# Windowed attention and a mixture of experts: the last token group's second GEMM by Strassen's scheme

## The chip, the cores and the metric

The kernel runs on one core of one Trainium2 chip. The metric is device time in microseconds of one execution, the median of the runs shown. TensorE (PE in the rows, PEld for its weight loads) does matrix products into PSUM; VectorE (DVE), ScalarE (ACT) and GpSimd (POOL) do the elementwise work; SyncE (SP) issues the DMAs.

## What is computed

The reference, cut to its core (batch 4, 8 heads, 576 tokens, head size 64; 2304 tokens of width 512; 4 experts with hidden width 1024):

```python
scores = scale * np.matmul(q, k.transpose(0, 1, 3, 2))
mask = (rel >= 0) & (rel < 64)
attn = softmax(np.where(mask, scores, -1e9))
x = np.matmul(attn, v).transpose(0, 2, 1, 3).reshape(2304, 512)
p = domain_probs / (domain_probs.sum(-1, keepdims=True) + 1e-9)
for e in range(4):
    h = np.maximum(x @ w1[e], 0.0)
    out += p[:, e:e + 1] * (h @ w2[e])
```

Every expert is applied to every token. Inputs and outputs are float32.

## The kernel before

**Precision.** Every big product is made of float32r operands in two parts: a rounded high part, and a low part, the rest. A product of 128 rows of weights is three matmuls: high x high, high x low, low x high.

**Groups and units.** The 2304 tokens are three groups of 768 (NGRP, numbered 0 to 2), each computed as two halves of 384 (T). The 4 x 1024 hidden columns are 16 units of 256 (NU), two row blocks of 128 each. So there are 48 units, `i` from 0 to 47; two neighbours are a pair. Attention for a group (18 steps of 128 tokens in all) runs beside the units of the group before; group 0's own attention is the start.

**First GEMM.** For a unit, the hidden values are a 2 x 2 block product (halves of the 512 input columns, halves of the hidden columns, halves of the tokens), done by Strassen's scheme in Winograd's form: seven products P1 to P7 (PROD, line 220 ff.), each six matmuls of 384 columns (L674). The combinations of x (B11, T1 and so on) are made once for a group, those of w1 for each unit (POOL, L536), and each is split into high and low (ACT L549, DVE L553). The products go to three PSUM banks: P1 and then P2 to X, P6, P7 and P4 to Y, P5 and P3 to V. P1 is copied to SBUF as s1 (ACT, L696); then DVE adds: u2 = Y + s1, u3 = Y + s1, c22 = V + u3, c21 = Y + s1, c12 = V + u2 (L693). The four results pass a relu and a split (`hidden`: ACT L600, DVE L603). The first two units are computed without Strassen (DIRECT). The order of the products in a unit is ORDER (P1, P6, P5, P7, P2, P4, P3), and FIRST (P1, P5, P2, P6, P7, P4, P3) in unit 2 and in the first and last unit of each group.

**Second GEMM.** For a pair and each of the group's six blocks of 128 tokens, y has 128 tokens x 512 columns: 6 matmuls of 512 columns for each of the two units (`gemm2`, L758), so 12 blocks of six a pair. w2 is loaded for each unit, cast and split (ACT L569, POOL L575). DVE adds p x y to an accumulator (L779), and after a group's last pair it is stored. The very last token block is done in two halves of 256 columns (`final`, L612 to L637).

**Order.** TensorE's steps stand in a list (`seq`): the products of a unit with a y block between each two, the y blocks two units behind. All other work has a due place against that list; a planner (`Planner.order`) that knows costs, buffers and the port that DVE and POOL share sets the order on every engine before the program is built. Each engine then runs its list in order, and waits at semaphores.

Of the kernel before, what the change touches and what calls it, by code (L numbers as in the profile page):

```python
# [44 lines left out]
class Planner:  # L45
# [5 lines left out]
    def order(self):  # L51
# [15 lines left out]
        while left:  # L67
# [60 lines left out]
def kernel(ctx: ExitStack, tc: tile.TileContext, q, k, v, dprobs, w1, w2, out):  # L128
    nc = tc.nc
    P = 128  # L130
    W = 64
    N, DM = out.shape
# [12 lines left out]
    NU = w1.shape[0]  # L145
    UPE = NU // E
# [17 lines left out]
    slots.update(X=["b0"], Y=["b1"], V=["b2"], D=["b0", "b1", "b2"], y=["b3", "b4"], pa=["b5", "b6", "b7"])  # L164
# [91 lines left out]
    for u in range(NG // 2):  # L256
# [66 lines left out]
        for c in range(2):  # L323
# [21 lines left out]
            else:  # L345
# [170 lines left out]
    w1p, w1_done, w2p, w2_done = {}, {}, {}, {}  # L516
    PIECES = (("w1a", 0, 2), ("w1b", 2, 4), ("w1c", 4, 6), ("w1d", 6, 7))
    COMBS = ((2, 1, 5, ALU.add), (3, 0, 1, ALU.subtract), (1, 2, 0, ALU.subtract), (6, 4, 1, ALU.subtract))
    for i in range(nun):
        ui = i % NU  # L520
        due = at["p", i, "P1"] - 7 if i >= DIRECT else -100 + 10 * i
        raw = Buf("w1r")

        def load_w1(on, i=i, ui=ui, b=raw):
            t = make(b, f"w1r{i}")
            nc.sync.dma_start(t[:, 0:2], w1[ui, :, 0:2])
            nc.sync.dma_start(t[:, 4:6], w1[ui, :, 2:4])

        ld = add(f"lw1_{i}", dict(SP=dma(524288)), load_w1, due - 14, takes=[raw])

        made = {}
        step = ld
        for dst, x, y, op in COMBS if i >= DIRECT else ():
            def comb_w1(on, b=raw, dst=dst, x=x, y=y, op=op):
                t = b.tile
                nc.gpsimd.tensor_tensor(out=t[:, dst], in0=t[:, x], in1=t[:, y], op=op)  # L536
# [353 lines left out]
```

## Time and profile before

| | |
|---|---|
| runs (us) | 836.97, 835.76, 837.24; median 836.97 |
| profiled execution: span | 833.3 us (the page gives no time of its own beside it) |
| TensorE busy | 816.3 us, 98% |
| DVE, ACT, POOL busy | 560.1, 355.4, 332.3 us (67%, 43%, 40%) |
| the chain that ended last | PE 93%, DVE 5% |
| costliest lines | L758 (second GEMM) 47% of the chain, L674 (first GEMM) 40% |
| DMA | 89.78 MB, mean 108 GB/s |

The span runs from the first to the last instruction; the timed runs are a little longer. Matmuls overlap in their pipeline, so the time of one is read from start to start. "Idle before" names what ended an engine's wait.

### The profile page before, as it was taken

To read this page: it belongs to the slowest core of one execution; us is meant where nothing else is said; L and a number is where in the kernel's file an instruction comes from. 1 tells how busy PE (TensorE), PEld (TensorE's weight loads), DVE (VectorE), ACT (ScalarE), POOL (GpSimd) and SP (SyncE) were. 2 spreads that over 40 slices of the span, in tenths; PEclk is the share of its full clock that TensorE was granted. 3 is DMA by queue.
4 is the path that set the end of the run, shared out by engine and by line. 5 is a ranking of instruction groups with operands and counts; after the bars stand their busy time and mean duration, and the time that the engine had idled before them with its cause. 6 is when DMAs were issued, how large, how long until landed. Compare 5 with 4: busy or idle time off the path is not lost.

```text
span 833.3 us, 13433 instructions
## 1 busy us (share of the span) xinstructions
PE 816.3 (98%) x5020; PEld 725.4 (87%) x5020; DVE 560.1 (67%) x966; ACT 355.4 (43%) x811; POOL 332.3 (40%) x339
## 2 busy tenths in 40 slices
PE   7988999999999999999999999999999999999998
PEld 6876988988888889888888888888889889889887
DVE  5868866665766797487688677588556566566553
ACT  5746535344453363464344443444353333333320
POOL 4744524344334254343435434425433433433400
PEclk8999999999999999999999999999999999999999
DMA  9633434343444235354343415114213113113102
GB/s 330 229 96 109 131 98 138 103 152 108 127 134 126 76 112 164 111 149 143 105 129 96 133 39 152 56 46 140 89 50 102 52 51 100 52 51 102 29 23 76
DMA packets 53521, 89.78 MB, mean 108 GB/s; under 512 B 8016, under 2 KB 20560, under 8 KB 53456
## 3 DMA queue, kind: packets, MB, share of 16 engines
q1 hardware_dynamic: 53312, 88.53, 33.4%
q8 instruction: 39, 0.64, 0.3%
q10 hardware_dynamic: 144, 0.39, 0.1%
q14 instruction: 26, 0.21, 0.1%
HBM read 77.89 MB, written 11.01 MB: 107 GB/s over the span
## 4 chain that ended last, share of the span: by engine, by line
PE 93%; DVE 5%; POOL 1%; issue 1%; ACT 0%; DMA 0%; DVEq 0%; POOLq 0%; ACTq 0%
PE y L758 47%; PE Y L674 17%; PE V L674 12%; PE X L674 11%; PE vb L436 2%; PE sb L311 2%; DVE T L479 1%; PE tb L386 1%; PE warm_out L801 1%; DVE h L603 0%; DVE w1c L553 0%; PE yl L627 0%; DVE B L479 0%; DMA qb<-in_q_dram 0%; ACT sm L339 0%
## 5 line engine op out<-in xcount | busy, mean ns | idle before, releaser
L758 PE MATMUL y<-w2s,h 128*128 128x512 f32 x1716 | 443.0, 394 | 1.4 <-POOL w2s L575 1.0
L758 PEld LDWEIGHTS y<-w2s,h 128*128 128x128 f32 x1716 | 317.5, 188 | 54.2 <-POOL w2s L575 1.8
L575 POOL TENSOR_TENSOR w2s<-w2r,w2s 128x512 fp32r<-128x512 f32 x96 | 134.1, 1409 | 212.5 <-ACT w2s L569 202.7
L536 POOL TENSOR_TENSOR w1r<-w1r 128x256 f32<-128x256 f32 x184 | 150.1, 821 | 168.5 <-DMA w1r<-in_moe_w_dram 143.9
L693 DVE TENSOR_TENSOR u<-Y,s 128x384 f32<-128x384 f32 x92 | 51.1, 555 | 124.1 <-PE Y L674 124.0
L779 DVE SCALAR_TENSOR_TENSOR acc<-y,dp,acc 128x512 f32<-128x512 f32 x125 | 93.1, 745 | 20.8 <-PE y L758 20.6
L603 DVE SCALAR_TENSOR_TENSOR h<-c,h 128x384 fp32r<-128x384 f32 x138 | 82.2, 603 | 15.8 <-ACT h L600 15.5
L600 ACT ACTIVATE h<-c 128x384 fp32r<-128x384 f32 x138 | 72.1, 525 | 24.9 <-DVE c L693 24.5
L549 ACT CAST w1b<-w1r 128x512 fp32r<-128x512 f32 x46 | 28.5, 620 | 112.8 <-PE Y L674 112.3
L377 POOL TENSOR_TENSOR sm<-sm,st 128x512 f32<-128x512 f32 x36 | 39.6, 1104 | 92.0 <-DVE st L371 79.7
L569 ACT CAST w2s<-w2r 128x1024 fp32r<-128x1024 f32 x48 | 50.4, 1050 | 25.5 <-PE y L758 21.3
L549 ACT CAST w1a<-w1r 128x512 fp32r<-128x512 f32 x48 | 29.8, 622 | 71.7 <-PE Y L674 66.8
L674 PE MATMUL V<-B,w1d 128*128 128x384 f32 x276 | 56.8, 341 | 1.6 <-DVE c L693 1.6
L674 PE MATMUL Y<-T,w1b 128*128 128x384 f32 x276 | 56.6, 340 | 0.0
L674 PE MATMUL V<-T,w1b 128*128 128x384 f32 x276 | 55.7, 336 | 0.9 <-DVE h L603 0.9
L674 PE MATMUL Y<-T,w1c 128*128 128x384 f32 x276 | 55.5, 336 | 0.8 <-ACT w1b L549 0.8
L674 PE MATMUL X<-B,w1c 128*128 128x384 f32 x276 | 56.2, 339 | 0.0
L674 PE MATMUL X<-B,w1a 128*128 128x384 f32 x276 | 55.4, 334 | 0.5 <-DVE h L603 0.5
L674 PE MATMUL Y<-T,w1a 128*128 128x384 f32 x276 | 55.4, 335 | 0.0
L693 DVE TENSOR_TENSOR c<-Y,s 128x384 f32<-128x384 f32 x46 | 25.5, 555 | 44.0 <-PE Y L674 43.9
L361 ACT ACTIVATE sm<-sm,st 128x128 f32<-128x128 f32 x120 | 46.6, 391 | 19.2 <-DVE st L354 19.0
L674 PEld LDWEIGHTS V<-B,w1d 128*128 128x128 f32 x276 | 49.8, 188 | 5.6 <-DVE c L693 1.9
(85 smaller groups left out, 973.7 us busy)
## 6 DMA issues: line engine op xcount, KB each, us to landing
w1r<-in_moe_w_dram SPq DMA_DIRECT2D x96, 256.0 KB, 3.7
w2r<-in_moe_w_dram SPq DMA_DIRECT2D x48, 512.0 KB, 3.6
vn<-in_v_dram SPq DMA_DIRECT2D x35, 256.0 KB, 3.0
kt<-in_k_dram SPq DMA_DIRECT2D x17, 384.0 KB, 4.9
hop<-tp SPq DMA_DIRECT2D x96, 64.0 KB, 1.8
pt<-hop SPq DMA_DIRECT2D x24, 256.0 KB, 2.9
qb<-in_q_dram SPq DMA_DIRECT2D x18, 256.0 KB, 4.0
out_dram<-acc SPq DMA_DIRECT2D x17, 256.0 KB, 2.0
```

What stands on the lines that cost most here:

```text
L361: nc.scalar.activation(t[:, p, :], t[:, p, :], AF.Exp, bias=st.tile[:, 1, p : p + 1], accum_out=st.tile[:, 2, p : p + 1],)
L377: nc.gpsimd.tensor_tensor(out=sm.tile, in0=sm.tile, in1=rl.to_broadcast([P, NP, P]), op=ALU.mult)
L536: nc.gpsimd.tensor_tensor(out=t[:, dst], in0=t[:, x], in1=t[:, y], op=op)
L549: f(t[:, 0], raw.tile[:, lo_:hi_])
L569: nc.scalar.copy(make(b, f"w2s{i}")[:, 0], raw.tile)
L575: nc.gpsimd.tensor_tensor(out=b.tile[:, 1, f], in0=raw.tile[:, f], in1=b.tile[:, 0, f].bitcast(F32), op=ALU.subtract)
L600: nc.scalar.activation(make(b, f"h{i}_{f}{t_}")[:, 0], src.tile[:, :T], AF.Relu)
L603: nc.vector.scalar_tensor_tensor(out=b.tile[:, 1], in0=src.tile[:, :T], scalar=0.0, in1=b.tile[:, 0].bitcast(F32), op0=ALU.max, op1=ALU.su ...
L674: nc.tensor.matmul(t[:, :T], wb.tile[:, a, wi, ws], cb.tile[:, x, c, :], start=first and m == 0, stop=m == 5, skip_group_check=True,)
L693: return lambda t, p_: nc.vector.tensor_tensor(out=t, in0=p_, in1=o.tile, op=ALU.add)
L758: nc.tensor.matmul(o, hh[:, a, ts], w[:, b, f, :], start=x == 0 and m == 0, stop=x == 1 and m == 5)
L779: nc.vector.scalar_tensor_tensor(out=ab.tile, in0=yb.tile, scalar=pc, in1=ab.tile, op0=ALU.mult, op1=ALU.add)
```

## The change

1. **Second GEMM of group 2, pairs 16 to 22.** It is computed transposed (w2 is the weight operand, the hidden values move) and by the same seven-product scheme over both units of a pair at once: blocks are halves of the 256 hidden columns of a unit, of the 512 output columns and of the 768 tokens. Each product is two blocks (`c`) of six matmuls of 384 columns, `gemm2m` (L993), three a unit. DVE (the first time ACT too) adds each block to one of 14 accumulators M (`gather`, L1007, L1009); the products are not combined until pair 22 is through (`total`).
2. **Weights for it.** While group 1 runs, the sums and differences of w2 that the scheme needs are made for 14 units (`w2_products`: POOL or DVE L607, ACT L614, L617), split and stored to DRAM, seven stores of 256 KB a unit; group 2 loads them, four loads a pair (`load_wp`, L693, L695).
3. **Split w1 kept.** Sixteen units (2 to 17) store w1a to w1d, already split, to DRAM (L574); group 2 loads them (`load_kept`, L561) in place of raw w1, and makes no combinations or splits of w1.
4. **Hidden values of group 2.** `weighted` (L813) applies relu and multiplies with the token's probability, which lies along columns now (probabilities are transposed once on TensorE and kept in DRAM, `prob_rows`); `minus` (L827) makes the differences, `cut` (L797, L800) the splits.
5. **The last pair, 23**, is not by Strassen: `gemm2z` (L1038), 14 blocks of six 384-column matmuls, then 24 of 192 columns. Output of group 2 is stored transposed, in a second tensor that the host turns back.
6. **P1 seeded into PSUM, in all groups.** ACT copies P1 from bank X into bank Y (L920) and P6, P7 and P4 accumulate there. So u2 and u3 are ACT copies out of Y, c21 is Y itself, and DVE has c22 and c12 left. P6 now waits for the seed.
7. The exps of the masked attention steps are two steps of two heads each instead of one of four; steps may be held back by a `gate` until TensorE's list has come to a place.

The diff, cut to its core:

```diff
+    MORDER = ("P1", "P3", "P7", "P5", "P6", "P2", "P4")
     def g_steps(pair, half):
+        if pair == nun // 2 - 1:
+            if half:
+                return []
+            full = [(dq, t) for t in (1, 0) for dq in range(DM // P)]
+            return [("z", pair, *x, y) for y in range(2) for x in full[:-1]] + [("zf", pair, *full[-1], y) for y in range(2)]
+        if pair >= LAST * NU // 2:
+            steps = [("m", pair, x, c) for x in MORDER for c in range(2)]
+            return steps[:7] if half == 0 else steps[7:]
         return [("g", pair, half * TPB + t, x) for t in range(TPB) for x in range(2)]
...
+    def keep_w1(i, kind, b, after, due):
...
+        def store(on):
+            nc.sync.dma_start(t, b.tile.bitcast(F32))
...
+        if i // NU == LAST:
+            for kind, lo_, hi_ in PIECES:
+                load_kept(i, kind, lo_, hi_, due - 2 + lo_)
...
+        if i // NU == LAST - 1 and ui < NU - 2:
+            w2_products(i, raw2, b2, w2_done[i])
...
-            first = pname in ("P1", "P6", "P5")
+            first = pname in ("P1", "P5")
...
-            elif pname == "P2":
+            elif pname in ("P2", "P6"):
                 after = after + [evac[i, "s1"]]
...
             if pname == "P1":
-                s1 = tmp("s1", lambda t, p_: nc.scalar.copy(t, p_), pb, [s], [], "ACT")
+                yb = bank[i, "Y"] = Buf("Y")
+
+                def seed(on, i=i, yb=yb, pb=pb):
+                    copy(on, make(yb, f"Y{i}")[:, :T], pb.tile[:, :T])
+
+                evac[i, "s1"] = add(f"s1_{i}", COPY, seed, due - 8, [s], [yb], [pb])
             elif pname == "P6":
-                u2 = tmp("u2", addto(s1), pb, [s, evac[i, "s1"]], [s1])
+                u2 = tmp("u2", copy, pb, [s], [], COPY, due=due - 8)
...
             elif pname == "P4":
-                c21 = tmp("c21", addto(s1), pb, [s, evac[i, "s1"]], [s1])
-                hidden(i, 1, 0, c21, [evac[i, "c21"]], due + 3, ("DVE",))
+                if i // NU == LAST:
+                    hidden_last(i, 1, 0, pb, [s], due, False)
+                else:
+                    hidden(i, 1, 0, pb, [s], due - 4)
...
+            def gemm2m(on, mb=mb, ww=ww, y=y, units=units, pname=pname, c=c, pair=pair):
+                o = make(mb, f"m{pair}{pname}{c}")
+                m = 0
+                for u, i in enumerate(units):
+                    for a, x in ((0, 0), (0, 1), (1, 0)):
+                        nc.tensor.matmul(
+                            o[:, :T], ww.tile[:, y, u, a, c * P : (c + 1) * P], hs[i, pname].tile[:, x], start=m == 0, stop=m == 5
+                        )
+                        m += 1
```

**The order on the engines.** TensorE, unit 40 of group 2, from its P1. Before (X, Y, V are the banks of the products, y the second GEMM, h the hidden values):

```order
L674 MATMUL X40_7111<-B11_2_5874,w1a_40_7018 128x384 x6
L758 MATMUL y19_0_7122<-w2s38_6895,h38_00_6945 128x512 x3
L758 MATMUL y19_0_7122<-w2s38_6895,h38_10_6967 128x512 x3
L674 MATMUL Y40_7141<-T2_2_5946,w1a_40_7018 128x384 x6
L758 MATMUL y19_0_7122<-w2s39_7087,h39_00_7077 128x512 x3
L758 MATMUL y19_0_7122<-w2s39_7087,h39_10_7100 128x512 x3
L674 MATMUL V40_7159<-T1_2_5897,w1b_40_7054 128x384 x6
```

and of the change (m19P10: pair 19, product P1, block 0; hs the split hidden values, wp the loaded w2 products):

```order
L899 MATMUL X40_7663<-B11_2_6298,w1a_40_7534 128x384 x6
L993 MATMUL m19P10_7677<-hs38P1_7456,wp19_0_7443 128x384 x3
L993 MATMUL m19P10_7677<-hs39P1_7613,wp19_0_7443 128x384 x3
L899 MATMUL Y40_7684<-T2_2_6377,w1a_40_7534 128x384 x6
L993 MATMUL m19P11_7701<-hs38P1_7456,wp19_0_7443 128x384 x3
L993 MATMUL m19P11_7701<-hs39P1_7613,wp19_0_7443 128x384 x3
L899 MATMUL V40_7715<-T1_2_6320,w1b_40_7563 128x384 x6
```

Between two products there is one block of six again; it has 384 columns instead of 512, and seven instead of six stand in a unit.

ACT around the copy of P1 at the start of unit 41 (of unit 40 before). Before:

```order
L549 CAST w1c_40_7095<-w1r40_6863 128x512
L600 ACTIVATE h39_10_7100<-c21_39_7097 128x384
L549 CAST w1d_40_7118<-w1r40_6863 128x256
L696 COPY s1_40_7132<-X40_7111 128x384
L600 ACTIVATE h39_01_7138<-c12_39_7120 128x384
```

and of the change (t40P5 is a difference of hidden values, hs40P5 its split):

```order
L797 CAST hs40P7_7816<-t40P7_7803 128x384 [waits Pool_49]
L797 CAST hs40P5_7828<-t40P5_7818 128x384 [waits DVE_49,Activation_49]
L920 COPY Y41_7839<-X41_7820 128x384 [waits PE_49]
L797 CAST hs40P2_7856<-c12_40_7812 128x384 [waits DVE_49]
L920 COPY u2_41_7867<-Y41_7839 128x384 [waits PE_49,Activation_49]
```

The copy writes a PSUM bank now, and the instruction ahead of it waits for DVE.

DVE in the change, from c12 of unit 40 on (MP50: accumulator of P5, block 0):

```order
L917 TENSOR_TENSOR c12_40_7812<-V40_7715,u2_40_7710 128x384 [waits PE_49]
L827 TENSOR_TENSOR t40P5_7818<-r4010_7794,c22_40_7753 128x384 [waits DVE_49]
L800 TENSOR_TENSOR hs40P7_7816<-t40P7_7803,hs40P7_7816 128x384 [waits Activation_49]
L827 TENSOR_TENSOR t40P6_7830<-r4000_7772,t40P5_7818 128x384 [waits DVE_49]
L800 TENSOR_TENSOR hs40P5_7828<-t40P5_7818,hs40P5_7828 128x384 [waits Activation_49]
L797 CAST hs40P6_7842<-t40P6_7830 128x384 [waits DVE_49]
L813 SCALAR_TENSOR_TENSOR c12_40_7812<-c12_40_7812,pb21_7646 128x384
L800 TENSOR_TENSOR hs40P6_7842<-t40P6_7830,hs40P6_7842 128x384 [waits DVE_49]
L827 TENSOR_TENSOR t40P4_7865<-c12_40_7812,t40P6_7830 128x384 [waits DVE_49]
L800 TENSOR_TENSOR hs40P2_7856<-c12_40_7812,hs40P2_7856 128x384 [waits Activation_49]
L1009 TENSOR_TENSOR MP50_6877<-m19P50_7805,MP50_6877 128x384 [waits PE_49]
```

Before, DVE had adds, subtractions of w1 and h, and three drains of y here, some 16 instructions a unit. From this c12 to that of unit 41 there are 24: c22 and c12, four weightings (two read PSUM), two casts, three differences, six subtractions and seven gathers. POOL has the fourth difference and the seventh subtraction. On SP, w1d of a unit waits for TensorE (P3 of the unit before), and w1a and w1b of the next unit stand behind it.

## Rows read from the trace of the kernel before

**Rows 1.** The view of the cores, and the chain's shares by engine (page).

```profile
core 0: 833.3 us, clock 0.994
...
PE 93%; DVE 5%; POOL 1%; issue 1%; ACT 0%; DMA 0%; DVEq 0%; POOLq 0%; ACTq 0%
```

**Rows 2.** Windows of groups 1 and 2: length, then busy time (instructions) per engine, clock, DMA.

```profile
296.00:561.00 265.00, 264.63 (x1601) 234.92 (x1600) 191.52 (x325) 118.24 (x272) 109.48 (x109) 1.00 0.36 110
561.00:812.00 251.00, 251.00 (x1251) 225.79 (x1250) 152.39 (x255) 95.00 (x168) 95.48 (x92) 1.00 0.21 70
```

**Rows 3.** Timeline of TensorE in group 2: start, length, engine, line, operation.

```profile
656.68 1.20 PE L674 MATMUL X<-B,w1a 128*128 128x384 f32 x6
657.72 1.55 PE L758 MATMUL y<-w2s,h 128*128 128x512 f32 x6
659.11 1.21 PE L674 MATMUL Y<-T,w1a 128*128 128x384 f32 x6
...
672.35 1.20 PE L674 MATMUL X<-B,w1a 128*128 128x384 f32 x6
```

**Rows 4.** Timeline of TensorE early in group 0.

```profile
91.60 1.21 PE L674 MATMUL Y<-T,w1b 128*128 128x384 f32 x6
...
95.79 1.21 PE L674 MATMUL X<-B,w1a 128*128 128x384 f32 x6
```

**Rows 5.** Timeline of TensorE at the end.

```profile
813.39 13.80 PE L758 MATMUL y<-w2s,h 128*128 128x512 f32 x60
827.03 3.03 PE L627 MATMUL yl<-w2s,h 128*128 128x256 f32 x24
```

**Rows 6.** Timeline around two s1 copies: one on time, the latest.

```profile
657.97 0.48 ACT L696 COPY s<-X 128x384 f32<-128x384 f32 x1 [0.61 <-PE X L674]
...
658.88 1.12 PEld L674 LDWEIGHTS Y<-T,w1a 128*128 128x128 f32 x6
...
625.33 1.20 PE L674 MATMUL X<-B,w1a 128*128 128x384 f32 x6
...
627.50 0.46 ACT L696 COPY s<-X 128x384 f32<-128x384 f32 x1
```

**Rows 7.** Groups of instructions in group 1, DVE and POOL: shapes, count, busy us, mean ns, idle before.

```profile
L603 DVE SCALAR_TENSOR_TENSOR h<-c,h 128x384 fp32r<-128x384 f32 x48 | 28.3, 600 | 4.4 <-ACT h L600 4.3
L693 DVE TENSOR_TENSOR u<-Y,s 128x384 f32<-128x384 f32 x32 | 17.7, 554 | 33.6 <-PE Y L674 33.6
L693 DVE TENSOR_TENSOR c<-V,u 128x384 f32<-128x384 f32 x32 | 17.6, 552 | 3.0 <-PE V L674 2.5
L553 DVE TENSOR_TENSOR w1c<-w1r,w1c 128x512 fp32r<-128x512 f32 x16 | 16.4, 1026 | 1.3
...
L553 DVE TENSOR_TENSOR w1a<-w1r,w1a 128x512 fp32r<-128x512 f32 x16 | 12.2, 760 | 1.8 <-ACT w1a L549 1.8
L693 DVE TENSOR_TENSOR c<-Y,s 128x384 f32<-128x384 f32 x16 | 8.9, 554 | 13.4 <-PE Y L674 13.4
...
L553 DVE TENSOR_TENSOR w1d<-w1r,w1d 128x256 fp32r<-128x256 f32 x16 | 7.7, 483 | 0.2 <-ACT w1d L549 0.2
...
L474 DVE CAST T<-xr 128x768 fp32r<-128x768 f32 x2 | 1.1, 554 | 0.1
...
L536 POOL TENSOR_TENSOR w1r<-w1r 128x256 f32<-128x256 f32 x64 | 53.8, 845 | 72.6 <-DMA w1r<-in_moe_w_dram 65.0 <-DVE acc L779 5.2
L575 POOL TENSOR_TENSOR w2s<-w2r,w2s 128x512 fp32r<-128x512 f32 x33 | 46.6, 1423 | 64.0 <-ACT w2s L569 59.0 <-DMA w1r<-in_moe_w_dram 5.0
```

**Rows 8.** Chain of waits between 76 and 84 us: start, length, what.

```profile
78.28 2.63 DMA qb<-in_q_dram
```

**Rows 9.** Windows of the start, and a line of the DMA issues (KB each, us to landing).

```profile
0.00:20.00 20.00, 14.98 (x200) 12.70 (x204) 10.79 (x31) 9.83 (x46) 9.72 (x23) 0.84 0.95 341
20.00:60.00 40.00, 35.44 (x418) 30.33 (x415) 29.51 (x53) 23.67 (x76) 25.31 (x25) 0.97 0.54 171
...
w1r<-in_moe_w_dram SPq DMA_DIRECT2D x96, 256.0 KB, 3.7
```

More of the change, by code (lines that the diff above doesn't have):

```diff
@@ L127, with kernel @@
 @with_exitstack
-def kernel(ctx: ExitStack, tc: tile.TileContext, q, k, v, dprobs, w1, w2, out):
+def kernel(ctx: ExitStack, tc: tile.TileContext, q, k, v, dprobs, w1, w2, out, out_t):
     nc = tc.nc
@@ L131 @@
     W = 64
-    N, DM = out.shape
+    DM, NL = out_t.shape
+    N = out.shape[0] + NL
     E = dprobs.shape[1]
@@ L154 @@
     for kind, n in dict(
-        qb=2, kt=2, vn=3, sm=3, tp=1, pt=3, hop=2, st=4, xr=1, w1r=2, w1a=1, w1b=1, w1c=1, w1d=1, w2r=1, w2s=3, h0=6, h1=8,
-        s1=1, u2=1, u3=1, c22=1, c21=1, c12=1, acc=TPB * 2, B11=1, B21=1, B22=1, T1=1, T2=1, T3=1, T4=1,
+        qb=2, kt=2, vn=3, sm=3, tp=1, pt=3, hop=2, st=4, xr=1, px=1, w1r=2, w1a=1, w1b=1, w1c=1, w1d=1, w2r=1, w2s=3, h0=6, h1=8,
+        u2=1, u3=1, c22=1, c12=1, acc=TPB * 2, B11=1, B21=1, B22=1, T1=1, T2=1, T3=1, T4=1,
     ).items():
@@ L184 @@
     )
-    for x in ("s1", "u2", "u3", "c22", "c21", "c12"):
+    for x in ("u2", "u3", "c22", "c12"):
         SHAPES[x] = ([P, T], F32)
@@ L521 @@
         due = at["p", i, "P1"] - 7 if i >= DIRECT else -100 + 10 * i
[L522 to L536, printed above, removed]
-            step = add(f"w1s{i}_{dst}", dict(POOL=0.75), comb_w1, due - 4, [step], [], [raw], port=("POOL",))
-            made[dst] = step
@@ new lines, in cut, with hi, lo @@
+    def cut(i, x, src, after, due):
+        b = hs[i, x] = Buf("hz")
+        def hi(on):
+            (nc.vector.tensor_copy if on == "DVE" else nc.scalar.copy)(make(b, f"hs{i}{x}")[:, 0], src.tile)
+        def lo(on):
+            (nc.gpsimd if on == "POOL" else nc.vector).tensor_tensor(
+                out=b.tile[:, 1], in0=src.tile, in1=b.tile[:, 0].bitcast(F32), op=ALU.subtract
+            )
+        h = add(f"zh{i}{x}", dict(ACT=act(T), DVE=dvec(T)), hi, due, after, [b], [src], port=("DVE",))
+        y = add(f"zl{i}{x}", dict(DVE=dve(T), POOL=pool_(T)), lo, due + 0.1, [h], [], [src, b], port=("DVE", "POOL"))
+        hs_done[i, x] = [h, y]
@@ L640, in final @@
-        uses = [y for i in units for y in (w2p[i], hb[i, 0, t_], hb[i, 1, t_])]
-        s = add(f"L{x}", dict(PE=12 * 0.118), gemm, due, after, [yb], [yb, *uses], seq=due)
-        dr = add(f"dL{x}", dict(DVE=0.42), drain, due + 1, [s, acc_step[NGRP - 1, t]], [], [yb, ab])
-        add(f"oL{x}", dict(SP=dma(131072)), store, due + 1, [dr], [], [ab])
+                out=src.tile if own else make(b, f"r{i}{f}{t_}"), in0=src.tile[:, :T], scalar=0.0, in1=pb.tile, op0=ALU.max, op1=ALU.mult
+            )
@@ new lines, in total, with emit @@
+    def total(n_, engine_due, a, b_):
+        for c in range(2):
+            def emit(on, c=c):
+                (nc.gpsimd if on == "POOL" else nc.vector).tensor_tensor(
+                    out=macc[a, c].tile, in0=macc[a, c].tile, in1=macc[b_, c].tile, op=ALU.add
+                )
+            mstep[a, c] = mdone[a, c] = add(
+                f"U{n_}{c}", dict(DVE=dve(T), POOL=pool_(T)), emit, engine_due, [mdone[a, c], mdone[b_, c], *mread.get((a, c), [])], [],
+                [macc[a, c], macc[b_, c]], port=("DVE", "POOL"),
+            )
+            mread.setdefault((b_, c), []).append(mdone[a, c])
```

372 lines of the change are left out of this document (301 added, 71 removed).

## Prediction

> **What bounds the kernel now.** First the view of the cores and the page's chain: the span is 833.3 us at a mean granted clock of 0.994, and TensorE holds 93% of the chain that ended last [rows 1]. The page does not list the profiled execution's own time. The three timed runs have a median of 836.97 us, 3.7 above the span; I take these 3.7 us as unchanged, work out the change of the span, and add it to the median. A measurement of this kernel can tell about 0.2%, 1.7 us, from no change.
>
> Next, the windows view. In group 1 (296 to 561 us) and group 2 (561 to 812) TensorE idles 0.4 us in 516, at a granted clock of 1.00, the upper of its two levels; VectorE (DVE) is busy for 191.5 of 265 and 152.4 of 251 us, ScalarE (ACT) for 118 and 95, GpSimd (POOL) for 109 and 95 [rows 2]. So TensorE's own stream is the time there, and only fewer or shorter matmuls shorten it; every other edit can only lose, unless it helps the start.
>
> How long is a matmul? The timeline of one unit of group 2 shows blocks of six matmuls. From the start of a product block of 384 columns to the next start is 1.04 us (656.68 to 657.72), after a y block of 512 columns 1.39 (657.72 to 659.11); a unit of seven products and six y blocks takes 15.67 (656.68 to 672.35) [rows 3]. Where 384-column blocks follow each other directly, four take 4.19 (91.60 to 95.79) [rows 4]. I use 1.39 and 1.045.
>
> **The change, part by part.** *Second GEMM of seven pairs.* Before, a pair is 12 y blocks: 12 x 1.39 = 16.68. After, it is 7 products x 2 column halves = 14 blocks of six 384-column matmuls: 14 x 1.045 = 14.63. That is -2.05 a pair, **-14.35** in all, fully on the path. The rows say that time follows columns: 1.39 / 6 = 232 ns and 1.045 / 6 = 174, a ratio of 0.75, that of the columns.
>
> The Trainium skill, "TensorE: Matmul & The Clock Gate", section "Back-to-back issue gap", speaks against this term: it gives a sustained spacing of about 81 ns at 128 columns and 131 at 512; a straight line between them gives, as an estimate, 114 ns at 384, and 84 x 114 = 9.6 us against 72 x 131 = 9.4, so no gain at all. Rows 3 and 4 disagree with that rule, and the sum goes by the rows.
>
> *Last pair.* Before, from the first y block (813.39) to the start of the last 24 matmuls of 256 columns (827.03) and their 3.03 us: 16.67 [rows 5]. After, 14 blocks, 14.63, and 24 matmuls of 192 columns, between 0.75 x 3.03 = 2.27 and 3.03; blocks are proportional in rows 3, so I take 2.4. Together **+0.4** (bounds +0.2 to +1.0). One transpose more on TensorE is priced as one matmul of rows 3, 0.17: **+0.2**.
>
> *Seed in PSUM.* s1 was a copy for DVE; now ACT writes it into bank Y, and P6, two blocks behind P1, waits for it. Before, P1's block ends at 657.88, the copy runs from 657.97 for 0.48, and the weight load of the block after next starts at 658.88: 0.43 us to spare [rows 3, 6]. The seed has the same spare in groups 0 and 1; in group 2 the block between is 0.345 shorter, and 0.085 is left. I measured all 46 copies of this kind in the timeline, from the end of P1's block to the copy's start: 39 start within 0.10 us, seven later, by 0.22, 0.26, 0.27, 0.54, 0.55, 0.84 and 0.97; rows 6 show the latest. What exceeds the usual 0.09 and the spare of 0.43 would have stalled P6 for 0.8 us in 46 units. ACT gets more work, so for the 26 units of groups 0 and 1 with this order I take **+1.0**. In group 2 the lateness seen there (0.45, 0.18 and 0.88) beyond 0.085 sums to **+1.3**. Bounds: nothing, and a mean lateness far above today's, priced as a rival.
>
> *DVE and POOL in group 2.* In the order shown ahead, DVE has 24 instructions a unit: c22, c12 and two weightings out of PSUM (0.55 each, as c<-V), two weightings in SBUF (0.60, as h<-c), two casts (0.28, half of a 768-column one), three differences (0.55, as u), six subtractions (0.60) and seven gathers (0.55) [rows 7]: 13.1 of 14.63 us, against 152.4 / 16 = 9.5 now. POOL has two, each between 0.85 (256 columns) and 1.42 (512) [rows 7]: 2.2 in all. The chain that counts is c12, t P5, its cast on ACT, and behind that cast, in ACT's order, the seed of the next unit. P3's block ends two blocks (2.09 us) ahead of P1's; c12, t P5 and the cast need 0.55 + 0.55 + 0.5. So 0.5 us of DVE's lateness is free, and 1.5 us a unit are there to catch up. I take **+0.7** for the group (bounds: nothing, and every POOL microsecond lost to DVE, rival B).
>
> *Group 1.* DVE loses u and c<-Y (17.7 and 8.9 us) and gains 90 operations of 256 columns at 0.48 [rows 7]: 191.5 - 26.6 + 43 = 208 of 265. POOL gains 22 x 0.85: 128. ACT gains 32 copies of 0.48 and 56 casts, shorter than those: at most 160. None is full. **+0.5**, near the 0.4 us that TensorE idles there now (bounds: nothing, and one wait of 2.63, as for a late qb [rows 8]).
>
> *Start.* Unit 2 sits behind DVE. Three adds of 0.55 leave it, and stores of w1 join SP's queue ahead of loads for attention. Between -1.7 (all three on the path) and +2.6 (one more late qb, rows 8) I take 0: no row is nearer to one end.
>
> *DMA.* SP stores split w1 for 16 units (128 x 3,584 floats, 1.84 MB each) and w2 products for 14 (1.84 MB), and reads both back in group 2. Of its new waits there, that of w1d is for P3 of the unit before, and the next unit's w1a and w1b stand behind it: a whole unit, 14.63 us, ahead of their use, where a 256 KB load lands in 3.7 [rows 9]. A unit needs 3.67 MB in 14.63 us, 251 GB/s; the first 20 us moved 341 [rows 9]. Cost 0 (bounds: nothing, and rival D).
>
> **Sum**: -14.35 + 0.4 + 0.2 + 1.0 + 1.3 + 0.7 + 0.5 = -10.25: span 823.05, median **826.7 us**.
>
> **The rivals.** *B. DVE paces group 2.* While POOL works, DVE's subtractions stretch: that into w1c has a mean of 1.03 us against 0.76 for w1a of the same shape [rows 7]. If POOL's 2.2 us all fall on DVE, a unit takes 13.1 + 2.2 = 15.3 instead of 14.63; over 14 units that is 9.4 more, in place of the 0.7 above: 835.4; half of it gives 830.7. Against it: operations that read PSUM, such as c<-V, show no stretch (0.55), and POOL's two can meet those. The Trainium skill, "SBUF — State Buffer", section "Terms", says that DVE and GpSimd lock a shared pair of ports for a whole instruction and the loser blocks fully; the row of w1c agrees. Chance 0.13.
>
> *C, slower: the seed on TensorE's path.* With a mean lateness L the 26 early units lose L - 0.43 each and 14 of group 2 L - 0.085. Without the seed terms the sum is -12.55, so this turns the sign from L = 0.62 on; at 0.75 the loss is 17.6 and the time 842. Against it: L is now 0.07, with ACT busy for 38% of group 2. For it: a cast that waits for DVE now stands directly ahead of the seed. Chance 0.08.
>
> *D, slower: DMA paces group 2.* It would have to stay under 3.67 MB in 15.67 us, 234 GB/s. From 20 to 60 us it moved 171, at a busy share of 0.54 [rows 9], so it was not pressed; if 171 were all, a unit would take 21.5 and the time would be near 920. Chance 0.04.
>
> *E. The weight load paces 384-column matmuls.* Six loads span 1.12 us [rows 6], 187 ns each. At that pace a block takes 1.12, the seven pairs gain 7 x (16.68 - 15.7) = 7, and the last pair costs 1.1 more: 835. Against it: rows 4, 174 ns with nothing between. The rule of the Trainium skill's "Back-to-back issue gap", that both weight load and matmul set the spacing, would lead this way. Chance 0.03.
>
> **How the numbers follow.** The forecast has 0.72. Its own bounds are all of the gain with the best start (-14.35 + 0.2 + 0.2 - 1.7: 821.3) and 4.5 us of additional stalls (831). The range for 8 in 10, **821.5 to 834.5**, takes in nearly all of the forecast and most of B. Faster by over 0.2% (below 835.3): the forecast, most of B, half of E: **0.84**. Within 0.2%: the rest of B and E, some of C: **0.06**. Slower: most of C, and D: **0.10**.
>
> **What would show it right or wrong.** In the changed profile: a step of 1.04 to 1.05 between m blocks; a unit of group 2 at 14.6 to 14.9; DVE near 90% busy from 561 us on with TensorE idle under 4 us there; waits of Y for ACT's copy of 1 to 3 us in total; a DMA share near 0.7 in group 2, and no wait of TensorE for w1a, w1b or wp. A unit of 15 us or more makes the prediction wrong, and its waits tell B (DVE), C (ACT's copy) and D (a DMA) apart; a step of 1.1 or more without a wait is E. Idle time above 3 us in group 1 also breaks the sum.

## The result, and the profile after

The change made the kernel 22 us faster: 814.28 us (median of 4 runs, 814.14 to 814.55) against 836.37 (835.07 to 837.24) beside it, a ratio of 0.9741 with an interval of 0.9725 to 0.9757. Predicted were 826.7, and 821.5 to 834.5 as the range. The direction was right; the gain is about twice the one forecast and lies outside the range.

The cores and the chain of the changed kernel, which answer to [rows 1]:

```profile
core 0: 812.7 us, clock 0.996
...
PE 98%; DVE 1%; ACT 0%; issue 0%; DVEq 0%; ACTq 0%
```

TensorE is now 98% of the chain, against 93%. Windows of the changed kernel (length, then busy time and instructions of PE, PEld, DVE, ACT and POOL, clock, DMA share, GB/s), which answer to [rows 2]; the last one covers twelve units of group 2:

```profile
50.00:100.00 50.00, 48.86 (x331) 43.91 (x330) 36.07 (x59) 30.71 (x75) 22.76 (x22) 1.00 0.74 246
296.00:561.00 265.00, 265.00 (x1628) 235.09 (x1627) 210.25 (x373) 139.99 (x348) 122.87 (x122) 1.00 0.68 224
...
592.00:767.00 175.00, 175.00 (x1010) 175.00 (x1009) 131.94 (x278) 50.98 (x107) 24.37 (x24) 1.00 0.75 261
```

TensorE never idles in group 1 or in these units of group 2, DVE is busy for 75% there (131.94 of 175), and the DMA engines moved 261 GB/s. The timeline of TensorE in one unit of group 2 (start, length, engine, line, operation), which answers to [rows 3]:

```profile
661.18 1.20 PE L899 MATMUL X<-B,w1a 128*128 128x384 f32 x6
662.22 0.68 PE L993 MATMUL m18P<-hs36P,wp 128*128 128x384 f32 x3
662.74 0.68 PE L993 MATMUL m18P<-hs37P,wp 128*128 128x384 f32 x3
663.26 1.20 PE L899 MATMUL Y<-T,w1a 128*128 128x384 f32 x6
...
675.76 1.20 PE L899 MATMUL X<-B,w1a 128*128 128x384 f32 x6
```

A product block and an m block take 1.04 each, and the unit 14.58 (661.18 to 675.76) against 15.67. The last pair, which answers to [rows 5]:

```profile
792.46 4.84 PE L1038 MATMUL z<-hs46P,w2s 128*128 128x384 f32 x27
...
807.02 0.47 PE L1038 MATMUL z<-hs46P,w2s 128*128 128x192 f32 x3
...
809.34 0.49 PE L1038 MATMUL z<-hs47H,w2s 128*128 128x192 f32 x3
```

From its first block to the end of the span it takes 812.7 - 792.46 = 20.24, before 833.3 - 813.39 = 19.91.

**Where the time came from.** Take two marks that both kernels have: the start of the product into V from w1b (P5's block) in unit 5, and the first block of the last pair.

| stretch | before | after | change |
|---|---|---|---|
| span's start to unit 5's block into V | 117.61 | 111.91 | -5.70 |
| from there to the last pair's first block | 695.78 | 680.55 | -15.23 |
| last pair to the end of the span | 19.91 | 20.24 | +0.33 |
| span | 833.3 | 812.7 | -20.6 |

So the second GEMM did what it was to do, no wait came in its place, and there are 5.7 us more at the start, where the prediction had put nothing. Below, a kernel's **start** is the time to that block of unit 5, and its **rest** the span less the start: 715.7 before, 700.8 after. Counted in the traces, TensorE has done the same matmuls ahead of the mark in both kernels but for one small transpose, so the 5.70 us are no work that moved behind it. Of the kernels below, b_exp and a_cost have the scores of one attention step (1.1 us) more ahead of the mark, and a_gate, a_noexp_gate and a_cost_gate one step's product with v (1.1 us) less. In the start I count the waits (idle time of TensorE up to 130 us) and, as low clock, what the granted clock took (the sum over windows of 2 us of one minus the granted clock, times 2). From before to the change the waits fall from 13.4 to 9.8 and the low clock from 5.1 to 3.4.

### The profile page after: what moved, and what is told of

It is laid out like the page before. It is cut to its first block, busy times and chain, and to the rows that moved or that the text cites. A ratio compares the mean times of both kernels' runs of the same rounds, so it can differ in the third digit from the quotient of the medians.

```text
span 812.7 us, 14283 instructions
## 1 busy us (share of the span) xinstructions
PE 800.1 (98%) x5129; PEld 734.3 (90%) x5129; DVE 588.1 (72%) x1091; ACT 359.8 (44%) x889; POOL 294.2 (36%) x301
## 4 chain that ended last, share of the span: by engine, by line
PE 98%; DVE 1%; ACT 0%; issue 0%; DVEq 0%; ACTq 0%
PE y L1076 33%; PE Y L899 18%; PE V L899 12%; PE X L899 12%; PE vb L472 2%; PE d L971 2%; PE z L1038 2%; PE sb L346 2%; PE m22P L993 2%; PE m21P L993 2%; PE m20P L993 2%; PE m19P L993 2%; PE m18P L993 2%; PE m16P L993 2%; PE m17P L993 2%; PE tb L422 1%
## 5 line engine op out<-in xcount | busy, mean ns | idle before, releaser
L1076 PE MATMUL y<-w2s,h 128*128 128x512 f32 x1152 | 298.3, 394 | 0.0
L1076 PEld LDWEIGHTS y<-w2s,h 128*128 128x128 f32 x1152 | 212.9, 188 | 34.8 <-issue 0.9
L658 POOL TENSOR_TENSOR w1r<-w1r 128x256 f32<-128x256 f32 x120 | 100.7, 846 | 72.9 <-DMA w1r<-in_moe_w_dram 64.8
L920 ACT COPY u<-Y 128x384 f32<-128x384 f32 x92 | 44.2, 480 | 168.9 <-PE Y L899 168.1
L917 DVE TENSOR_TENSOR c<-V,u 128x384 f32<-128x384 f32 x92 | 51.0, 554 | 86.7 <-ACT u L920 78.1
L899 PEld LDWEIGHTS Y<-T,w1b 128*128 128x128 f32 x276 | 48.9, 188 | 3.6 <-ACT u L920 0.9
L899 PEld LDWEIGHTS Y<-T,w1a 128*128 128x128 f32 x276 | 49.0, 188 | 3.4 <-ACT Y L920 0.7
L899 PEld LDWEIGHTS Y<-T,w1c 128*128 128x128 f32 x276 | 48.6, 188 | 3.8 <-ACT u L920 0.9
L899 PEld LDWEIGHTS V<-T,w1b 128*128 128x128 f32 x276 | 49.0, 188 | 2.9 <-issue 0.2
L899 PEld LDWEIGHTS X<-B,w1c 128*128 128x128 f32 x276 | 49.2, 188 | 2.6
```

The lines of the kernel that those rows point to most:

```text
L899: nc.tensor.matmul(t[:, :T], wb.tile[:, a, wi, ws], cb.tile[:, x, c, :], start=first and m == 0, stop=m == 5, skip_group_check=True,)
L917: return lambda on, t, p_: nc.vector.tensor_tensor(out=t, in0=p_, in1=o.tile, op=ALU.add)
L920: (nc.vector.tensor_copy if on == "DVE" else nc.scalar.copy)(t, p_)
L1076: nc.tensor.matmul(o, hh[:, a, ts], w[:, b, f, :], start=x == 0 and m == 0, stop=x == 1 and m == 5)
```

## The experiments

**First set: which part speeds up the start?** Theory X: the split exponentials. Theory S: the seed. Theory L: no part by its own doing; every edit gives the planner another list, and the start that falls out of it is short or long. A planner's *list* is the order of work that it puts on each engine. All four kernels are the kernel before with the edits shown (their core lines).

```diff
 b_exp and b_both
-                e = add(f"e{uc}", dict(ACT=4 * (0.46 + 0.00083 * P)), exps, due + 1.5, [m], [], [sm, st])
+                e = None
+                for lo in range(0, NP, 2):
...
+                    e = add(f"e{uc}{lo}", dict(ACT=2 * (0.46 + 0.00083 * P)), exps, due + 1.5, [m, e], [], [sm, st])
 b_seed and b_both
-            first = pname in ("P1", "P6", "P5")
+            first = pname in ("P1", "P5")
...
+                evac[i, "s1"] = add(f"s1_{i}", COPY, seed, due - 8, [s], [yb], [pb])
 b_jit
-                step = add(f"w1s{i}_{dst}", dict(POOL=0.75), ...
+                step = add(f"w1s{i}_{dst}", dict(POOL=0.76), ...
```

b_exp. 

> The kernel before with one part of the change: the four exponentials of a softmax step as two steps of two. In the change the seventh TensorE block of unit 5 of its start (first block into V of unit 5) came 5.70 us earlier, 111.91 against 117.61, and the prediction had put the start at nothing. Theory X (the split exponentials shorten the softmax chains of the start): 1.5 to 2.5 us earlier there, since 1.9 us of the gain was there before unit 2's first product; time about 834.3. Theory S (the seed takes DVE out of unit 2): nothing from this part, time within 1 us of before. Theory L (it is not a part's own doing: any edit gives the planner's list another order at the start, with another time): the block moves by 1 to 3 us either way.

b_seed. 

> The kernel before with the seed alone: P1 copied by ACT into PSUM bank Y, u2 and u3 as ACT copies, c21 gone, P6 waiting for the copy; second GEMM, w1 and w2 as before. Theory S: unit 2's waits for DVE (0.46, 0.94 and 1.61 us before) and the one for w1b (0.83) go, two waits of 0.57 for the seed come: 2.7 to 4 us earlier at unit 5, time 832 to 834. Theory X: no gain at the start. The prediction's own terms (1.0 us of seed stalls in groups 0 and 1, 1.3 in group 2, start 0): 1 to 2.5 us slower than before. Theory L: a start that differs by 1 to 3 us either way.

b_both. 

> The kernel before with the split exponentials and the seed. If S and X hold and add up: the first block into V of unit 5 at about 112 and the time 830.5 to 831.5, the whole 5.7 us of the start without any of the second GEMM. If only one holds, the time of that one alone. Theory L: any start between the two, not the sum of the two single parts.

b_jit. 

> The kernel before with one number of the planner's table changed, the cost of a w1 sum on POOL 0.76 instead of 0.75, and nothing of what is computed: only the order of the instructions can move. Theories S and X: time within 1 us of before. Theory L: the start moves by 1 to 3 us either way, and with it the time.

| kernel | median us | ratio to before, interval | span | start | rest | waits | low clock |
|---|---|---|---|---|---|---|---|
| before | 835.8 | | 833.3 | 117.61 | 715.7 | 13.4 | 5.1 |
| b_exp | 827.78 | 0.991 (0.9893 to 0.9927) | 826.7 | 112.64 | 714.1 | 9.1 | 5.1 |
| b_seed | 833.96 | 0.9979 (0.9967 to 0.999) | 832.7 | 117.67 | 715.0 | 14.1 | 5.1 |
| b_both | 827.11 | 0.9901 (0.9885 to 0.9916) | 825.5 | 110.92 | 714.6 | 8.8 | 5.1 |
| b_jit | 834.74 | 0.9995 (0.9984 to 1.0006) | 835.9 | 119.64 | 716.3 | 14.8 | 6.8 |

The split exponentials shorten the start: alone they give 8.0 us of the median, 5.0 of them in the start, and the seed hardly moves it. The split stood in the change (its point 7), and the prediction did not price it at all. The median of the kernel before went from 835.1 to 836.4 us over the sets of runs, so a difference of about 1 us between two sets says little. b_jit says nothing on theory L, since its list is the same as before's throughout the start; it shows instead how far a start varies with one list (see the end).

ACT's timeline tells what the split lets happen. Before (start, length, engine, line, operation):

```profile
25.00 0.40 ACT L361 ACTIVATE sm<-sm,st 128x128 f32<-128x128 f32 x1
...
26.17 0.39 ACT L361 ACTIVATE sm<-sm,st 128x128 f32<-128x128 f32 x1
26.46 0.19 ACT L361 ACTIVATION_READ_ACCUMULATOR sm<-sm,st 128x1 f32 x1
27.35 0.83 ACT L474 CAST B<-xr 128x768 fp32r<-128x768 f32 x1 [0.70 <-DVE xr L449]
```

and in b_exp:

```profile
24.04 0.39 ACT L363 ACTIVATE sm<-sm,st 128x128 f32<-128x128 f32 x1
...
25.25 0.58 ACT L451 COPY xr<-vb 128x512 f32<-128x512 f32 x1 [0.74 <-PE vb L438]
25.87 0.83 ACT L476 CAST B<-xr 128x768 fp32r<-128x768 f32 x1
26.61 0.40 ACT L363 ACTIVATE sm<-sm,st 128x128 f32<-128x128 f32 x1
```

The copy of xr, DVE's before, goes to ACT between two halves. ACT's cast of B starts 1.48 us earlier, and the first matmul of group 0, which waits for DVE's cast of B, 0.91 (27.11 against 28.02). Later the cast of w1a for unit 2 follows two exponentials instead of four (60.12 against 63.16), and two more of the attention's chains of four exponentials are done ahead of unit 2 (36 exponentials against 28). Unit 2 begins at 64.72 instead of 67.33, and takes 13.4 us instead of 17.0.

**Second set: is it the room between the halves, or the planner's price?** The planner holds four exponentials for 2.27 us; the rows above show 1.65 (25.00 to 26.65). b_cost corrects the price and leaves the step whole. Of the other three, two take a part out of the changed kernel, and a_due moves the due place of ACT's copies to that of their product. a_noseed also has one order edge more, among the w2 sums.

```diff
 b_cost
-                e = add(f"e{uc}", dict(ACT=4 * (0.46 + 0.00083 * P)), exps, ...
+                e = add(f"e{uc}", dict(ACT=4 * (0.31 + 0.00083 * P)), exps, ...
 a_due (u2 and u3 likewise)
-                evac[i, "s1"] = add(f"s1_{i}", COPY, seed, due - 8, [s], [yb], [pb])
+                evac[i, "s1"] = add(f"s1_{i}", COPY, seed, due, [s], [yb], [pb])
 a_noseed
+                s1 = tmp("s1", copy, pb, [s], [], COPY)
...
+                u2 = tmp("u2", addto(s1), pb, [s, evac[i, "s1"]], [s1], SUM)
```

b_cost. 

> The kernel before with the four exponentials left as one step, and only the planner's price for that step changed, from 2.27 us to 1.66 us, which is what the four take in the trace of before (25.00 to 26.65 us). Theory X1 (the gain of the split exponentials, 8.0 us of the median, comes from what can stand between two halves): no gain, within 1.5 us of before. Theory X2 (the step of four was priced too long, so the plan put ACT's other work, the copy of xr and the cast of B, in a wrong place): the xr copy now goes to ACT as it does with the split, and the time is 828 to 830. Between the two, 831 to 834: both.

a_noexp (the split of b_exp taken back). 

> The changed kernel with the four exponentials as one step again. If the split is worth here what it is worth alone (8.0 us at the median, 6.6 of span): 820 to 822. If the other parts (gate, seed) already keep ACT free at the start: 814 to 816. In both cases group 2 stays at 14.58 us a unit without a wait of TensorE.

a_noseed. 

> The changed kernel without the seed: s1 goes to SBUF as before, u2, u3 and c21 are DVE's again, P6 opens Y. The prediction had the seed cost 2.3 us, so by it 812. By the run of the seed alone (0.6 us of span, 1.8 of the median gained): 814.5 to 816. If group 2 needs it, because DVE's 77% there rises by three adds of 0.55 us a unit, to 27 instructions: TensorE waits for DVE in group 2, 816 to 822.

a_due. 

> The changed kernel with the ACT copies Y, u2 and u3 due at their product's own place instead of 8 blocks earlier, so that the list may put a cast or an exponential ahead of them, as it did for s1 before. Theory: the seed did not stall because the plan puts it first (copies of group 2 all start 0.19 to 0.20 us after the next block's start). Then here some start late and TensorE waits for ACT, 1 to 3 us in all: 815 to 817. Rival: ACT is free enough in any order: within 1 us of 814.3, no new wait.

| kernel | median us | ratio to before, interval | span | start | rest | waits | low clock |
|---|---|---|---|---|---|---|---|
| changed | 814.28 | 0.9741 (0.9725 to 0.9757) | 812.7 | 111.91 | 700.8 | 9.8 | 3.4 |
| b_cost | 833.72 | 0.9982 (0.9972 to 0.9991) | 831.9 | 116.74 | 715.2 | 12.8 | 5.1 |
| a_noexp | 818.63 | 0.9804 (0.9789 to 0.9819) | 817.1 | 114.69 | 702.4 | 13.3 | 1.7 |
| a_noseed | 816.07 | 0.9772 (0.9756 to 0.9789) | 814.3 | 112.16 | 702.1 | 10.4 | 3.4 |
| a_due | 818.76 | 0.981 (0.9793 to 0.9827) | 816.8 | 111.61 | 705.2 | 10.9 | 1.7 |

b_cost moves the copy of xr to ACT as the split does, and the last direct block of group 0 comes at 63.88 instead of 65.66; but unit 2 then waits 2.2 us for h, and 1.4 us of the median is all that is left. In the changed kernel the split is worth 4.4 us, not 8.0, so the parts don't add up.

The seed, priced at a loss of 2.3 us, loses nothing: without it the median is 1.8 us longer, TensorE waits 0.8 us for DVE's u in one place after 100 us, and the rest is 1.3 longer. That it gains is not shown, since other lists that keep the seed have rests of 700.8 to 705.2. ACT has room for it. Its timeline in group 1 of the changed kernel:

```profile
357.70 0.39 ACT L397 ACTIVATE sm<-sm,st 128x128 f32<-128x128 f32 x1
...
358.08 0.47 ACT L920 COPY Y<-X 128x384 f32<-128x384 f32 x1
358.49 0.40 ACT L397 ACTIVATE sm<-sm,st 128x128 f32<-128x128 f32 x1
```

This seed stands between two halves and ends at 358.55, a microsecond ahead of P6 (359.55). TensorE's waits for ACT's copies in the whole start, first of the changed kernel, then of a_due (view of the waits: in total, times, longest):

```profile
PE Y L899 <- ACT u L920: 1.1, 2, 0.6
...
PE Y L899 <- ACT u L920: 2.3, 2, 1.1
```

My theory on a_due, that only the early due keeps the copies from stalling TensorE, holds for a small part. The late due costs 1.1 us more of waits for u in unit 2, and 0.3 us for one seed after 130 us; in group 2 the seeds of both kernels start 0.20 us after the next block's start at the latest, the copies of u 0.25. But a_due's start is no longer (111.61), and it is 4.5 us slower for another reason: its list has changed behind the start too. In the first unit of group 1 DVE has w2 sums and a w1 split ahead of c. DVE's timeline in a_due:

```profile
304.18 1.51 DVE L607 TENSOR_TENSOR tw16P<-tw16P,w2r 128x256 f32<-128x256 f32 x1
...
306.45 1.39 DVE L675 TENSOR_TENSOR w1b<-w1r,w1b 128x512 fp32r<-128x512 f32 x1
307.76 0.54 DVE L917 TENSOR_TENSOR c<-V,u 128x384 f32<-128x384 f32 x1
```

and what TensorE makes of it:

```profile
308.36 1.35 PE L899 MATMUL V<-B,w1d 128*128 128x384 f32 x6 [1.85 <-DVE c L917]
309.51 2.12 PE L899 MATMUL X<-B,w1a 128*128 128x384 f32 x6
```

The same two operations of DVE, and POOL's beside the second, in the changed kernel:

```profile
298.98 0.41 DVE L607 TENSOR_TENSOR tw16P<-tw16P,w2r 128x256 f32<-128x256 f32 x1
...
301.59 2.49 POOL L658 TENSOR_TENSOR w1r<-w1r 128x256 f32<-128x256 f32 x2
...
302.79 0.69 DVE L675 TENSOR_TENSOR w1b<-w1r,w1b 128x512 fp32r<-128x512 f32 x1
```

The w2 sum takes 0.41 us there, with POOL idle, and 1.51 in a_due, where POOL works from 301.52 on without a gap; the split takes 0.69 and 1.39. POOL works beside the split in both kernels, and in the changed one it is POOL's sums that take longer, 1.24 each. The wait of 1.85 us brings 1.7 of low clock with it (0.95 granted over 296 to 330 us): most of the 4.4 that the rest grew.

**Third set: a finer split, another price, POOL left out.** If room between the steps is what counts, four steps of one do at least as well as two of two.

```diff
 b_exp4 and a_exp4 (each step priced at one exponential; a_exp4 with the order edge of a_noseed)
-                for lo in range(0, NP, 2):
+                for lo in range(0, NP, 1):
 a_cost
-                    e = add(f"e{uc}{lo}", dict(ACT=2 * (0.46 + 0.00083 * P)), exps, ...
+                    e = add(f"e{uc}{lo}", dict(ACT=2 * (0.31 + 0.00083 * P)), exps, ...
 a_nopool (lo of cut; minus likewise)
-        y = add(f"zl{i}{x}", dict(DVE=dve(T), POOL=pool_(T)), lo, ...
+        y = add(f"zl{i}{x}", dict(DVE=dve(T)), lo, ...
```

b_exp4. 

> The kernel before with the four exponentials as four steps of one. Split in two they gave 8.0 us, and the price alone 1.4. Theory X1 (finer steps let the plan put a softmax chain of the start into ACT's gaps ahead of unit 2): at least what two halves gave, 826 to 828. Theory L (the order that two halves happened to give is a lucky one): back to 830 to 835.

a_exp4. 

> The changed kernel with the four exponentials as four steps of one (and one order edge more among the w2 products, which the list needs). Theory X1: 812.5 to 814.5. Theory L: 816 to 820, as without the split or with the copies in another place (818.6 and 818.8).

a_cost. 

> The changed kernel with the planner's price of two exponentials 0.83 us, as they take in the trace, instead of 1.13. If the price matters by itself, as it did in the kernel before (1.4 us): 812 to 814. Theory L: anywhere within 4 us of 814.3.

a_nopool. 

> The changed kernel with the subtractions of the last group's y for DVE alone, so POOL has none of them. By the trace of the changed kernel DVE starts one 384-column operation every 0.47 us and is busy 75% of 592 to 767 us; two more a unit are 0.94 us of 14.58, 82%: no wait of TensorE, 814 to 815. By the prediction's way of counting (0.55 us each, 13.1 of 14.6 us with 24): 14.2 of 14.58, so waits of 0.5 us a unit or more, 816 to 824.

| kernel | median us | ratio to before, interval | span | start | rest | waits | low clock |
|---|---|---|---|---|---|---|---|
| b_exp4 | 834.36 | 0.9979 (0.9969 to 0.9989) | 832.5 | 117.22 | 715.3 | 13.2 | 6.8 |
| a_exp4 | 818.38 | 0.9785 (0.9769 to 0.9801) | 816.6 | 114.70 | 701.9 | 11.0 | 6.8 |
| a_cost | 821.08 | 0.9813 (0.9793 to 0.9833) | 819.7 | 118.89 | 700.8 | 11.0 | 10.2 |
| a_nopool | 814.25 | 0.974 (0.9725 to 0.9754) | 813.0 | 111.79 | 701.2 | 9.2 | 5.1 |

Theory X1 (room between the steps) falls. Four steps of one lose nearly all of it, in both kernels, and the price that helped the kernel before costs the changed one 6.8 us. The rests of these three changed kernels hardly move (700.8 to 701.9); their starts run from 111.8 to 118.9. By these runs what the two halves gave is the start that their list happens to have.

a_nopool settles rival B, by which DVE paces group 2. DVE takes both of POOL's operations and nothing changes. The timeline of DVE in group 2 of the changed kernel shows why:

```profile
663.42 0.56 DVE L800 TENSOR_TENSOR hs38P<-t38P,hs38P 128x384 fp32r<-128x384 f32 x1
663.89 0.55 DVE L827 TENSOR_TENSOR t38P<-c,t38P 128x384 f32<-128x384 f32 x1
664.36 0.55 DVE L800 TENSOR_TENSOR hs38P<-c,hs38P 128x384 fp32r<-128x384 f32 x1
```

An operation is listed with 0.55 us, and the next begins after 0.47: 24 of them make 11.3 us, not the 13.1 that the prediction counted. (In the twelve units of the window above DVE has 278 instructions, 23 a unit.)

**Fourth set: one feature of the start?** Unit 2 of the kernel before waits 3.84 us, and work of group 1's attention stands inside it (TensorE's timeline):

```profile
67.33 1.31 PE L674 MATMUL X<-B,w1a 128*128 128x384 f32 x6 [0.46 <-DVE h L603]
...
70.98 1.31 PE L674 MATMUL V<-T,w1b 128*128 128x384 f32 x6 [0.94 <-DVE h L603]
...
77.09 1.10 PE L311 MATMUL sb<-kt,qb 64*64 64x128 f32 x32
...
80.27 1.28 PE L674 MATMUL Y<-T,w1c 128*128 128x384 f32 x6 [0.83 <-ACT w1b L549]
83.16 1.31 PE L674 MATMUL V<-B,w1d 128*128 128x384 f32 x6 [1.61 <-DVE c L693]
```

Theory G says that this attention costs the time. These kernels hold it back in the plan until unit 3.

```diff
 b_gate (with the changed kernel's gate in its planner), a_gate, a_noexp_gate, a_cost_gate
         s = add(f"S{u}", dict(PE=1.15 + 0.44 * pe_mask), scores, due, ...
+        if n == 1:
+            s.gate = at["p", 3, "P1"]
```

b_gate. 

> The kernel before, with group 1's scores held back in the plan until unit 3's first product; exponentials unsplit, nothing else changed. Theory G (group 1's softmax chains inside unit 2 cost the time: unit 2 waits 3.84 us for DVE and ACT there): unit 2 takes about 13 us from its first product to unit 3's, as in the changed kernel (13.17), instead of 16.98; time 829 to 832. Rival (the waits of unit 2 come from the x and w1 splits that DVE has there anyway): unit 2 over 16 us, time within 1.5 us of 836.

a_gate. 

> The changed kernel with the same hold. Its unit 2 waits only 1.1 us, for ACT's u. Theory G: 813 to 815, at best the 1.1 us gained. Rival: as any new order, up to 7 us slower.

a_noexp_gate. 

> The changed kernel with unsplit exponentials (818.6 us) and the hold. Theory G: the 3.7 us that its unit 2 waits mostly go, 814.5 to 816.5. Rival: 817.5 to 820.

a_cost_gate. 

> The changed kernel with the price of 0.83 us for two exponentials (821.1 us, its unit 2 takes 20.9 us) and the hold. Theory G: 814 to 816. Rival (the low clock, 10.2 us lost to it in the first 100 us against 3.4, has another cause): above 818.

| kernel | median us | ratio to before, interval | span | start | rest | waits | low clock |
|---|---|---|---|---|---|---|---|
| b_gate | 836.4 | 1.0011 (1.0 to 1.0023) | 834.9 | 119.08 | 715.8 | 14.9 | 5.1 |
| a_gate | 817.13 | 0.9781 (0.9763 to 0.9799) | 815.7 | 113.60 | 702.1 | 12.3 | 3.4 |
| a_noexp_gate | 819.23 | 0.9809 (0.9794 to 0.9823) | 817.1 | 113.50 | 703.6 | 12.4 | 3.4 |
| a_cost_gate | 818.69 | 0.9797 (0.9778 to 0.9816) | 816.5 | 112.60 | 703.9 | 11.7 | 3.4 |

Theory G falls too. Unit 2's waits do go (in b_gate from 3.84 to 1.39 us), but others come: there the second set of direct blocks waits 2.6 us for DVE's work on B instead of 1.5, and a y block 2.0 for h. a_cost_gate gains 2.4, a_gate loses 2.9, a_noexp_gate and b_gate are the same as without the hold. So the attention inside unit 2 does not carry the start; a start is the sum of all its waits and of the clock behind them, and each list has its own.

One thing does go with the short starts in all the profiles. In the six kernels that start in 110.9 to 112.6 us (changed, b_exp, b_both, a_noseed, a_due, a_nopool) 36 exponentials are done ahead of unit 2; in the nine without a hold that take 114.7 to 119.6 it is 28 or 32, and with the hold 24 (112.6 to 119.1). No run changes this number alone, so whether it is the cause is not shown.

**Last: the second GEMM alone.** a_neither has neither the seed nor the split.

> The changed kernel without the seed and with unsplit exponentials: the second GEMM of the last group, its stored sums and the kept w1 alone. From the first block into V of unit 5 to the end of the span the kernel before takes 715.7 us, the changed one 700.8, and without the seed 702.1. If the GEMM alone carries the gain behind the start: 701.5 to 703 from that block to the end; the start, by theory L, anywhere between 111 and 119. Time 816 to 823. By the prediction's sum without the two seed terms: 12.55 less than before, 823.5 from 836.0.

It took 821.96 us (0.9833, 0.981 to 0.9855), span 821.3, start 118.94 (waits 17.2, low clock 1.7), rest 702.4. The rest is 13.3 us shorter than before's, with the seed and the split 14.9; the start is a poor one. So the transposed Strassen GEMM, with the loads that it needs, carries 13.3 of the 20.6 us, and the start 5.7. The 1.6 that are left stand behind the start; they may be the seed's and the split's, or the list's, since rests of the changed kernel differ by up to 4.4 with the list alone.

No kernel tried beats the changed one; a_nopool equals it.

## Why the prediction was wrong, point by point

- **What bounds the kernel: right.** TensorE's stream; it is now 98% of the chain.
- **Second GEMM, -14.35: right, a little small.** The step came out at 1.04 us (1.045 was used), the unit at 14.58 instead of 14.63, and the stretch to the last pair shrank by 15.23; with neither seed nor split (a_neither) the rest is 13.3 shorter. The sustained spacing that the Trainium skill, "TensorE: Matmul & The Clock Gate", section "Back-to-back issue gap", gives, and by which there was no gain, does not hold here: three 384-column matmuls take 0.52 us (662.22 to 662.74), 173 ns each, in proportion to the 232 of 512 columns.
- **Last pair, +0.4: right**, +0.33. The 24 matmuls of 192 columns take 0.333 us for three, 111 ns each, between the two bounds.
- **Seed in PSUM, +1.0 and +1.3: wrong, it cost nothing behind the start.** I applied the lateness of the old copies beyond the spare. In the changed kernel the only waits for ACT's copies are two of 0.57 us for u in unit 2; in group 2 every seed is on time, and with the late due (a_due) one wait of 0.3 came after 130 us. Taking the seed out gives nothing back (a_noseed is 1.8 slower). The step counted ACT's old load, with softmax in group 1 and casts of w1 and w2 in group 2, and did not see that group 2 loses those casts: ACT is busy for 29% there (50.98 of 175) against 38% before.
- **DVE and POOL in group 2, +0.7: wrong, nothing.** The count was near (23 and 2 a unit), the 13.1 us were not: durations overlap, and DVE is 75% busy, not near 90%.
- **Group 1, +0.5: wrong, nothing.** DVE's 208 was 210.25, POOL's 128 was 122.87, ACT's 140 stayed under 160; no wait appeared, and the 0.4 us of idle went.
- **Start, 0 with -1.7 to +2.6: wrong, -5.7.** This is the largest miss. The step looked at the adds and at SP's queue, and left out the exponentials, whose split gives the start 5.0 us alone (b_exp against before). No row would have given the number; but the bounds should have been those of a new list. The starts measured here on lists that differ run from 110.9 to 119.1. The shortness is in part luck: four steps of one, or another price for the same two halves, lose 2.8 and 7.0 us of it. Why this list starts early stays open.
- **Time and span: wrong by 1.8.** Every run has its time 1.7 to 2.1 us above its span (814.55 and 812.7; 837.64 and 835.9). By that the profiled execution before took about 835.1 us, not the median of 836.97; taking 3.7 as constant moved the forecast up.
- **The rivals.** B, C, D and E all stayed out: no wait for DVE, ACT or a DMA after 100 us, a step of 1.04 us, and 261 GB/s where 251 were needed.

Sum of the misses in the span: 5.7 for the start, 3.5 for waits that did not come, 0.4 for idle that went, 0.6 for the finer step (14 units by 0.045): 10.2 of the 10.35 between -10.25 and -20.6.

## What to carry to other kernels

Where a planner writes the order, an edit can deal the start anew: a part that computes the same in smaller steps moved it by 5 us, and the same idea taken further gave it back. Give such a stretch bounds from runs of other lists, not from the instructions that it gains or loses, and measure a change apart from it, from a mark behind the start. Before applying a wait's statistics to a new instruction, look whether the edit also changes the load of the engine that made it wait. And take an engine's load from the distance between starts, not from the sum of durations.

## What the runs showed of the hardware

A wait in the start can cost more than itself. TensorE in unit 2 of a_cost (timeline):

```profile
80.43 2.29 PE L899 MATMUL V<-B,w1d 128*128 128x384 f32 x6 [1.84 <-DVE c L917]
82.52 2.12 PE L899 MATMUL X<-B,w1a 128*128 128x384 f32 x6
84.44 2.51 PE L1076 MATMUL y<-w2s,h 128*128 128x512 f32 x6
```

and windows of the same stretch:

```profile
78.00:80.00 2.00, 0.59 (x4) 0.27 (x2) 2.00 (x5) 1.89 (x9) 0.00 (x0) 0.92 0.69 240
80.00:82.00 2.00, 1.57 (x5) 1.57 (x6) 1.59 (x3) 2.00 (x11) 0.00 (x0) 0.50 1.03 422
82.00:84.00 2.00, 2.00 (x8) 2.00 (x7) 1.25 (x3) 1.28 (x4) 0.00 (x0) 0.50 0.91 349
```

From the end of the wait on the granted clock is 0.50, the lower level of 1.2 GHz, for three blocks that take 6.35 us instead of 3.47 (1.04, 1.04 and 1.39). The low clock's cost in the starts above is always near a multiple of 1.7 us: 1.7, 3.4, 5.1, 6.8 or 10.2. It is not fixed by the list: before and b_jit run the same list in the start, both wait 1.61 us for c in unit 2, and the clock fell in that wait in b_jit alone. The windows that follow, before and then b_jit:

```profile
84.00:86.00 2.00, 2.00 (x12) 1.91 (x11) 2.00 (x6) 1.25 (x4) 0.00 (x0) 1.00 0.12 31
...
84.00:86.00 2.00, 2.00 (x7) 2.00 (x8) 1.36 (x3) 0.33 (x2) 0.00 (x0) 0.50 0.00 0
```

From the block behind the wait to the next block into V b_jit takes 7.47 us and before 6.01, which is most of the difference of the starts (119.64 against 117.61). The runs of b_jit go from 834.2 to 837.6; from 130 to 767 us, where TensorE hardly waits, the clock is 1.00 in every profile but a_due's.
